# A gated dilated convolution on one core: another order of the matmul groups in even and odd units, and a tail with early row transposes, ScalarE casts and a split last store

## The chip, the cores and the metric

The kernel runs on one core of one Trainium2 chip. The metric is the device time of one execution in microseconds (us), as the median of several runs. The profile is of one more execution, with its own time.

## The reference

Two sequences of 16000 steps with 144 channels go through a causal convolution with 15 taps two steps apart (`pad` is 28, `dil` 2), which gives 288 channels. The first 144 pass through tanh, the last 144 through a sigmoid, the two are multiplied, and the product is multiplied by a 144 x 144 matrix.

```python
B, T, D, K = (2, 16000, 144, 15)     # x [B,T,D], w [K,D,2D], w_o [D,D], bfloat16
dil = 2
pad = (K - 1) * dil
xp = jnp.pad(x, ((0, 0), (pad, 0), (0, 0)))
h = jnp.einsum('btc,cd->btd', xp[:, pad:pad + T, :], w[0])
for i in range(1, K):
    off = pad - i * dil
    h = h + jnp.einsum('btc,cd->btd', xp[:, off:off + T, :], w[i])
f = h[..., :D].copy()
g = h[..., D:].copy()
z = jnp.tanh(f) * _sigmoid(g)
return z @ w_o
```

## The kernel before, in words

**Tiling.** The 32000 steps are cut into 128 pieces of 250, one for each partition of an output tile. Eight neighbouring steps of all pieces make an octet ("oct", `o`); octets are handled in pairs `o0`, `o1`, 15 pairs, and each pair in two units, one for each parity `r`. So 30 units make the main loop (lines 1257 to 1288); even `u` is `r` = 0. The channels are split into 128 (tiles named XA, and V, DU, DD, GX, GU, GV, GD, made from it by subtractions on VectorE) and 16 (XB, BD, packed eight taps to a tile). The 15 taps are not computed one by one: sums and differences of tiles and weights share products between neighbouring outputs. Every matmul of the convolution has 288 output columns and one PSUM bank as its target.

**The parts of a unit**, with their names in `ORDER`. A unit holds banks in pairs.

- CV, CD, XC, XR and SR (lines 973 to 1048) compute for the next unit (`v` = `u` + 1) what its outputs have in common. CV starts a bank with a common product and ScalarE copies the bank (line 967); CD adds to it, and ScalarE evicts it to UD or UC. XC starts a bank and copies it, XR adds to it; its first half (k = 0) is read by VectorE (line 994, into a table kept in Xp), its second half (k = 1) by ScalarE into XS. SR starts the pair of banks p for each of the two octets (h = 0, 1).
- UP (line 1002) adds XS and UC on GpSimd (Pool) into UX.
- EF(u, h) (line 1050) adds the products of GV to the pair p, and VectorE then adds (line 1068) the tables to it: with Xp into a new pair n (k = 0), with UX back into p (k = 1).
- DD(u, h, k) (line 1071) adds six or five products of GD and BD to n (k = 0) or p (k = 1). `halves` then has ScalarE write sigmoid and tanh of the two banks to TG, and VectorE multiplies them (`gate`, line 848). In all units but the last the product goes to Z, both k at once, in `finish`.
- PJ is one of the projections that wait in `todo` (line 913): the octet in Z has been transposed to ZT by a DMA from SP's queue (`ship`, line 908), matmuls with the output matrix (WOR, line 925) make its rows, ScalarE casts them into OS (line 929), and SP stores the octet (line 935). An octet has three groups.

**The tail.** The last unit's gates cannot wait for a transposing DMA. For the last two octets, positions 0, 2, 4 and 6 come from the unit before; they are transposed by DMA and projected by `project_some` (line 938). The last unit's gates go to ZL, a zero-padded area in Xr, and `ship_pair` (line 873) takes two positions at a time (`dl` 7 stands for 5 and 7, `dl` 3 for 1 and 3): three TensorE transposes (line 880), a copy to SBUF (ZTL, in Xr, line 883, helper line 871), three matmuls (line 885), a cast into OS (line 889, helper line 871). `store_some` (line 894) stores an octet.

**What sets the order.** Nothing runs in the order of the calls. Each call adds an operation with an engine, a modelled duration, what it reads and writes, and its place in the list (its index). A planner (`schedule`, line 110, and `run`, line 152) then fills the engines in model time and fixes each engine's order. TensorE takes, of the operations that are ready, the one with the lowest index, no further ahead than `PE_WIN` operations; operations marked `floating` come after all others. An operation that opens a bank may do so only if enough of the eight banks are left for openers with lower indices (`may_open`, line 193). The other engines rank by how late an operation may be by the passes before. SP's queue and its DMAs are planned in the same way. `ORDER` has two strings, for even and odd units, which say in which order the calls are made, and so the indices. `soft` makes an operation start no earlier than another has started, in the plan alone.

Of the kernel before, what the change touches and what calls it, by code (L numbers as in the profile page):

```python
# [5 lines left out]
ACT = mybir.ActivationFunctionType  # L6
# [4 lines left out]
NP = 128  # L11
# [4 lines left out]
PE_WIN = 42  # L16
ORDER = ("EF0 PJ DD00 EF1 XC1 DD01 CV DD10 CD0 XC0 CD1 DD11 XR0 SR0 PJ SR1 PJ XR1 UP0 UP1", "EF0 PJ EF1 XC1 CV DD01 DD00 XC0 CD0 CD1 DD10 SR0 DD11 XR1 XR0 UP0 UP1 SR1 PJ PJ")
# [357 lines left out]
def _conv_wavenet_kernel(nc, x, w, w_o, out):  # L375
    B, T, D = x.shape
# [18 lines left out]
    NPAIR = NOCT // 2  # L395
# [19 lines left out]
    with contextlib.ExitStack() as st:  # L415
# [4 lines left out]
        Xr = sb("Xr", [NP, NX, XCH, D], BF16)  # L420
# [417 lines left out]

        def halves(b, b2, s, k):

            for h, fn in enumerate((ACT.Sigmoid, ACT.Tanh)):
                def th(a, h=h, fn=fn):
                    return evict(a, TG, NTG * 8 * D, ((s * 2 + h) * 4 + 2 * k) * D, D, b, b2, (1 - h) * D, fn)
                g.add("act", th, r=[("bank", b), ("bank", b2)], w=[("TG", s, k, h)], dur=0.31, prio=0)

        def gate(s, k, n, dst, key, dur):

            g.add("dve", lambda v: v.tensor_tensor(dst(), TG[:, s, 1, 2 * k:2 * k + n, :], TG[:, s, 0, 2 * k:2 * k + n, :], ALU.mult),  # L848
                  r=[("TG", s, q, h) for q in range(k, k + n // 2) for h in range(2)], w=key, dur=dur, lock=True)
# [17 lines left out]
        tl_n = [0]  # L867
        last_store = {}

        def cast(eng, dst, src):  # L870
            return (lambda e: e.activation(dst(), src(), ACT.Copy)) if eng == "act" else (lambda e: e.tensor_copy(dst(), src()))  # L871

        def ship_pair(o, h, dl, eng):

            q = tl_n[0] % 4
            os_ = (o + 1) % NO
            tl_n[0] += 1
            pa, bo = _Bank(), _Bank()
            c0 = h * 672 + (dl - 3) // 2 * D
            g.add("pe", [lambda t, i=i: t.transpose(PSb[:, pa.phys * 1024 + 128 * i:pa.phys * 1024 + 128 * i + 128], ZL[:, c0 + 128 * i:c0 + 128 * i + 128], ID[:]) for i in range(3)],  # L880
                  r=[("ZL", h, 3), ("ZL", h, 7), "ID"] if dl == 3 else [("ZL", h, 7), "ID"], w=[("bank", pa)], dur=0.2, floating=True)
# [3 lines left out]
            fns = [lambda t, i=i, c=c, w=w, n=n: t.matmul(PS[:, bo.phys * 512 + c:bo.phys * 512 + c + n * D], lhsT=ZTL[:, q, 128 * i:128 * i + 128],  # L885
                                                          rhs=WOR[:, w:w + n, :].rearrange("p a b -> p (a b)"), start=i == 0, stop=True, skip_group_check=True)
                   for i, c, w, n in ((0, 0, 0, 1), (1, 0, 1, 2), (2, D, 3, 1))]
            g.add("pe", fns, r=[("ZTL", q)] + wor_keys, w=[("bank", bo)], dur=0.3, floating=True)
            op = g.add(eng, cast(eng, lambda: bass.AP(OS[:].tensor, (os_ * 8 + dl - 2) * D, [[NO * 8 * D, NP], [2 * D, 2], [1, D]]),
                                 lambda: PS[:, bo.phys * 512:bo.phys * 512 + 2 * D].rearrange("p (a b) -> p a b", a=2)),  # L890
                       r=[("bank", bo)], w=[("OS", os_, dl)], dur=0.4)
            op.deps.add(last_store[os_])

        def store_some(o, dls, step, n, d0):
            os_ = (o + 1) % NO
            def f(e):
                src = bass.AP(OS[:].tensor, (os_ * 8 + d0) * D, [[NO * 8 * D, NP], [step * D, n], [1, D]])
                dst = bass.AP(out_t, (KD + 8 * o + d0) * D, [[L * D, NP], [step * D, n], [1, D]])
                return e.dma_start(dst, src)
            g.add("sp", f, r=[("OS", os_, d) for d in dls] + [("OS", os_, d, h) for d in dls for h in range(2)], w=[], dur=0.5, dma="st", nbytes=NP * n * D * 2)  # L900
# [12 lines left out]
        def project(o, gi):  # L913
# [15 lines left out]
            g.add("act", lambda e: e.activation(OS[:, os_, a:c, :].rearrange("p e d -> p (e d)"), PS[:, bo.phys * 512:bo.phys * 512 + (c - a) * D], ACT.Copy),  # L929
# [8 lines left out]
        def project_some(o, dls, eng):  # L938

            zt, os_ = (o + 1) % NZT, (o + 1) % NO  # L940
            for h, part in enumerate((dls[:3], dls[3:])):
                b = _Bank()
                fns = []
                for i, dl in enumerate(part):
                    for k in range(2):
# [5 lines left out]
                           r=[("bank", b)], w=[("OS", os_, 0, h)], dur=0.05 + len(part) * D / 1200.0)  # L951
# [119 lines left out]
        def DD(u, h, part):  # L1071
# [20 lines left out]
            gate(s, k, 2, lambda: bass.AP(Xr[:].tensor, XCH * D + c, [[NX * XCH * D, NP], [-D, 2], [1, D]]), [("ZL", h, dl)], 0.22)  # L1092

# [285 lines left out]
```

## Time and profile before

| | us |
|---|---|
| median of 3 runs | 310.57 (310.0 to 312.39) |
| the profiled execution | 310.4 |
| its span, first to last instruction | 308.7 |
| busy in the span: TensorE matmuls | 301.6 |
| VectorE | 289.9 |
| ScalarE | 258.4 |
| GpSimd | 99.6 |

PE is TensorE's matmuls, PEld its weight loads, DVE VectorE, ACT ScalarE, POOL GpSimd, SP the engine whose queue ("SPq") issues the DMAs. A row of the timeline has a start in us from the start of the span, a length in us, engine, line, operation, output <- inputs, shapes, count, and in brackets the idle time before it and what ended it. Neighbouring instructions of a kind are merged. A matmul's shown duration (286 ns for 288 columns) includes its way through the pipeline; in a row without waits the next starts 0.12 us after it. So "PE busy" hides small waits, and the number of matmuls in a stretch tells more. Lines in Z, ZL, ZTL and the table of UE appear under the names of the memory they lie in: ZL and ZTL as Xr, UE as Xp.

### The profile page before, as it was taken

Reading aid. Unit: us, or ns where it says so; the run is one execution under the profiler, and the core shown is the slowest. Engines: PE = TensorE matmul, PEld = TensorE weight load, DVE = VectorE, ACT = ScalarE, POOL = GpSimd, SP = SyncE. Lnnn points to the kernel's source line nnn. Section 1 sums busy time; section 2 is a strip of 40 time slices with the busy share of each in tenths; the row PEclk is TensorE's granted clock in tenths of the full one; section 3 lists DMA queues with packets and bytes.
Section 4 is the critical chain, followed back from the end, with each engine's and each line's share of the span. In section 5 each row is a group of like instructions: output and inputs, shape, how many; then the busy total and the mean of one; then the engine's idle time right before and its main releaser. Section 6 shows DMA issues by size and latency. Waiting matters only on the chain.

```text
span 308.7 us, 7536 instructions
## 1 busy us (share of the span) xinstructions
PE 301.6 (98%) x2569; PEld 235.6 (76%) x2569; DVE 289.9 (94%) x652; ACT 258.4 (84%) x812; POOL 99.6 (32%) x89
## 2 busy tenths in 40 slices
PE   7999999999999999999999999999999999999995
PEld 7787677778877788787776788777788877778884
DVE  1999899999999999999999999999999999999864
ACT  3376788988888998888898888899888889888884
POOL 7480332133333223333321333331233332223330
PEclk9999999999999999999999999999999999999999
DMA  7956657789476883757695476739646783372342
GB/s 212 289 123 148 147 161 187 116 168 162 169 153 155 190 220 101 156 183 170 124 235 165 121 157 173 205 84 236 179 113 146 161 211 99 101 173 71 86 118 115
DMA packets 100241, 48.48 MB, mean 157 GB/s; under 512 B 88269, under 2 KB 90893, under 8 KB 100203
## 3 DMA queue, kind: packets, MB, share of 16 engines
q1 hardware_dynamic: 99657, 47.62, 62.8%
q0 software_dynamic: 512, 0.33, 0.5%
q8 instruction: 20, 0.33, 0.5%
q14 instruction: 18, 0.15, 0.2%
q10 hardware_dynamic: 34, 0.05, 0.1%
HBM read 13.77 MB, written 10.20 MB: 78 GB/s over the span
## 4 chain that ended last, share of the span: by engine, by line
PE 82%; DVE 6%; ACT 4%; SPq 3%; DMA 2%; issue 1%; POOL 0%; DVEq 0%; ACTq 0%
PE PS L823 73%; PE PS L925 9%; DMA WA<-in_w_dram 2%; ACT TG L475 1%; ACT PS L967 1%; SPq L708 1%; DVE V L731 1%; SPq L517 1%; DMA XB<-s 1%; DVE DD L731 1%; DVE DU L731 1%; DVE OS L871 1%; POOL UX L1004 0%; DVE WC L666 0%; SPq L696 0%
## 5 line engine op out<-in xcount | busy, mean ns | idle before, releaser
L1004 POOL TENSOR_TENSOR UX<-UC,XS 128x576 f32<-128x576 f32 x60 | 83.7, 1417 | 194.0 <-ACT UC L478 149.4
L823 PE MATMUL PS<-WA,GD 128*128 128x288 bf16 x450 | 87.6, 286 | 0.2
L967 ACT ACTIVATE PS<-PS 128x288 f32<-128x288 f32 x213 | 80.1, 433 | 0.4
L475 ACT ACTIVATE TG<-PS 128x288 bf16<-128x288 f32 x170 | 60.6, 422 | 15.9 <-PE PS L823 15.8
L823 PE MATMUL PS<-WB,BD 128*128 128x288 bf16 x240 | 67.5, 286 | 0.0
L929 ACT ACTIVATE OS<-PS 128x432 bf16<-128x432 f32 (+1 forms) x88 | 41.8, 491 | 13.6 <-PE PS L925 13.2
L823 PEld LDWEIGHTS PS<-WA,GD 128*128 128x128 bf16 x450 | 40.8, 98 | 16.0 <-DVE PS L1068 3.3
L1068 DVE TENSOR_TENSOR PS<-PS,Xp 128x288 f32<-128x288 f32 x120 | 49.4, 457 | 1.9 <-PE PS L823 0.5
L1068 DVE TENSOR_TENSOR PS<-PS,UX 128x288 f32<-128x288 f32 x120 | 49.3, 455 | 0.0
L823 PE MATMUL PS<-WS,GU 128*128 128x288 bf16 x210 | 44.6, 286 | 0.4 <-DMA XB<-XB 0.2
L994 DVE TENSOR_TENSOR Xp<-PS,UD 128x576 f32<-128x576 f32 x60 | 42.7, 750 | 2.1 <-ACT UD L478 1.7
L925 PE MATMUL PS<-WOR,ZT 128*128 128x144 bf16 (+1 forms) x322 | 41.1, 253 | 0.0
L478 ACT ACTIVATE TG<-PS 128x144 bf16<-128x144 f32 x160 | 33.8, 311 | 5.1 <-PE PS L823 5.0
L823 PE MATMUL PS<-WB,XB 128*128 128x288 bf16 x140 | 37.6, 286 | 0.0
L823 PE MATMUL PS<-WC,GV 128*128 128x288 bf16 x210 | 35.7, 286 | 0.3 <-ACT PS L967 0.3
L925 PEld LDWEIGHTS PS<-WOR,ZT 128*128 128x128 bf16 x322 | 27.9, 98 | 5.5
L823 PE MATMUL PS<-WD,DD 128*128 128x288 bf16 x210 | 31.0, 286 | 0.0
L848 DVE TENSOR_TENSOR Z<-TG 128x576 bf16<-128x576 bf16 (+1 forms) x63 | 27.5, 438 | 2.9 <-ACT TG L478 2.0
L823 PEld LDWEIGHTS PS<-WB,BD 128*128 128x128 bf16 x240 | 23.5, 98 | 5.7
L823 PEld LDWEIGHTS PS<-WS,GU 128*128 128x128 bf16 x210 | 20.4, 98 | 7.3 <-ACT PS L967 1.9
L823 PEld LDWEIGHTS PS<-WD,DD 128*128 128x128 bf16 x210 | 19.7, 98 | 6.5 <-ACT PS L967 1.3
L823 PE MATMUL PS<-WT,DU 128*128 128x288 bf16 x120 | 24.5, 286 | 0.0
(93 smaller groups left out, 476.2 us busy)
## 6 DMA issues: line engine op xcount, KB each, us to landing
out_dram<-OS SPq DMA_DIRECT2D x31, 288.0 KB, 2.6
Xr<-in_x_dram SPq DMA_DIRECT2D x15, 576.0 KB, 4.7
XB<-XB SPq DMA_DIRECT2D x30, 192.0 KB, 2.7
XB<-s SPq DMA_DIRECT2D x59, 32.0 KB, 2.2
s<-T SPq DMA_DIRECT2D x30, 32.0 KB, 2.3
WA<-in_w_dram SPq DMA_DIRECT2D x2, 288.0 KB, 5.0
ZT<-Z SPq DMA_TRANSPOSE x32, 2.9
Xp<-in_x_dram SPq DMA_DIRECT2D x2, 252.0 KB, 4.6
```

The lines of the kernel that those rows point to most:

```text
L475: return e.activation(bass.AP(t[:].tensor, off + (0 if st > 0 else n), [[row, NP], [st, 2], [1, n]]), bass.AP(PS[:].tensor, lo * 512 + c0, ...
L478: ins = e.activation(bass.AP(t[:].tensor, off + i * n, [[row, NP], [1, n]]), bass.AP(PS[:].tensor, q.phys * 512 + c0, [[8 * 512, NP], [1, ...
L517: return e.dma_start(tile_ap, src)
L731: return g.add("dve", lambda v: v.tensor_tensor(dst(), a(), b(), ALU.subtract), r=r, w=wk, dur=dur, prio=2, lock=True)
L823: return lambda t: t.matmul(bank(b), lhsT=lhs(), rhs=rhs(), start=start, stop=True, skip_group_check=True)
L848: g.add("dve", lambda v: v.tensor_tensor(dst(), TG[:, s, 1, 2 * k:2 * k + n, :], TG[:, s, 0, 2 * k:2 * k + n, :], ALU.mult), r=[("TG", s, ...
L925: return t.matmul(PS[:, c0:c0 + n * D], lhsT=ZT[:, zt, blk_, :], rhs=WOR[:, wi_:wi_ + n, :].rearrange("p a b -> p (a b)"), start=first, st ...
L929: g.add("act", lambda e: e.activation(OS[:, os_, a:c, :].rearrange("p e d -> p (e d)"), PS[:, bo.phys * 512:bo.phys * 512 + (c - a) * D], ...
L967: g.add("act", lambda e: e.activation(bank(c), bank(b), ACT.Copy), r=[("bank", b)], w=[("bank", c)], dur=0.29, prio=prio)
L994: return v.tensor_tensor(ue(u % NU, q, 0, 2).rearrange("p (v n) -> p v n", v=2), src, UD[:, u % NUD, :, :], ALU.add)
L1004: op = g.add("pool", lambda p: p.tensor_tensor(UX[:, u % NU, h, :, :], UC[:, 0, :, :], bass.AP(XS[:].tensor, h * N2, [[2 * N2, NP], [0, 2] ...
L1068: g.add("dve", lambda e, dst=dst, src=src, ua=ua: e.tensor_tensor(bank(dst), bank(src), ua(), ALU.add), r=[("bank", src), ("UX", us, h) if ...
```

## The change

The strings of `ORDER` are replaced, and `PE_WIN` goes from 42 to 50. The three row transposes and the copy to SBUF leave `ship_pair` and become `ship_rows`, which is called right behind each gate of the last unit; its copies are all on VectorE, and neither transposes nor projections are `floating` any more. The casts of `project_some` and `ship_pair` of o0 go to ScalarE and those of `ship_pair` of o1 to VectorE; the last group of the third-to-last octet's projection (octet 28) goes from ScalarE to VectorE. `project_some` splits its four positions 2 and 2 instead of 3 and 1, and its casts start, in the plan, no earlier than the last eight `halves`. The last octet is stored in two pieces of four steps. Some modelled durations change too.

```diff
-PE_WIN = 42
-ORDER = ("EF0 PJ DD00 EF1 XC1 DD01 CV DD10 CD0 XC0 CD1 DD11 XR0 SR0 PJ SR1 PJ XR1 UP0 UP1", "EF0 PJ EF1 XC1 CV DD01 DD00 XC0 CD0 CD1 DD10 SR0 DD11 XR1 XR0 UP0 UP1 SR1 PJ PJ")
+PE_WIN = 50
+ORDER = ("EF0 PJ EF1 XC1 CV CD0 XC0 CD1 XR0 DD00 SR0 XR1 PJ DD11 UP0 DD01 PJ UP1 SR1 DD10", "EF0 PJ EF1 DD00 XC1 CV CD0 DD01 CD1 XC0 DD10 XR1 UP0 SR0 DD11 PJ XR0 UP1 SR1 PJ")
...
+        lasts = []
...
-                g.add("act", th, r=[("bank", b), ("bank", b2)], w=[("TG", s, k, h)], dur=0.31, prio=0)
+                lasts.append(g.add("act", th, r=[("bank", b), ("bank", b2)], w=[("TG", s, k, h)], dur=0.31, prio=0))
...
-        def ship_pair(o, h, dl, eng):
-
-            q = tl_n[0] % 4
-            os_ = (o + 1) % NO
-            tl_n[0] += 1
-            pa, bo = _Bank(), _Bank()
+        def ship_rows(h, dl):
+
+            q = 2 * h + (dl == 3)
+            pa = _Bank()
             c0 = h * 672 + (dl - 3) // 2 * D
             g.add("pe", [lambda t, i=i: t.transpose(PSb[:, pa.phys * 1024 + 128 * i:pa.phys * 1024 + 128 * i + 128], ZL[:, c0 + 128 * i:c0 + 128 * i + 128], ID[:]) for i in range(3)],
-                  r=[("ZL", h, 3), ("ZL", h, 7), "ID"] if dl == 3 else [("ZL", h, 7), "ID"], w=[("bank", pa)], dur=0.2, floating=True)
-            old = set(g.readers[("Xr", 0)])
-            a = g.add(eng, cast(eng, lambda: ZTL[:, q, 0:384], lambda: PSb[:, pa.phys * 1024:pa.phys * 1024 + 384]), r=[("bank", pa)], w=[("ZTL", q)], dur=0.4)
-            a.deps |= old
+                  r=[("ZL", h, 3), ("ZL", h, 7), "ID"] if dl == 3 else [("ZL", h, 7), "ID"], w=[("bank", pa)], dur=0.2)
+            a = g.add("dve", lambda e: e.tensor_copy(ZTL[:, q, 0:384], PSb[:, pa.phys * 1024:pa.phys * 1024 + 384]), r=[("bank", pa)], w=[("ZTL", q)], dur=0.27)
+            a.deps |= set(g.readers[("Xr", 0)])
+
+        def ship_pair(o, h, dl, eng):
+
+            q = 2 * h + (dl == 3)
+            os_ = (o + 1) % NO
+            bo = _Bank()
...
-            g.add("pe", fns, r=[("ZTL", q)] + wor_keys, w=[("bank", bo)], dur=0.3, floating=True)
+            g.add("pe", fns, r=[("ZTL", q)] + wor_keys, w=[("bank", bo)], dur=0.25)
...
-                       r=[("bank", bo)], w=[("OS", os_, dl)], dur=0.4)
+                       r=[("bank", bo)], w=[("OS", os_, dl)], dur=0.37 if eng == "dve" else 0.29)
...
+            eng = "dve" if (o, gi) == (2 * NPAIR - 2, 2) else "act"
...
-            for h, part in enumerate((dls[:3], dls[3:])):
+            for h, part in enumerate((dls[:2], dls[2:])):
...
-                           r=[("bank", b)], w=[("OS", os_, 0, h)], dur=0.05 + len(part) * D / 1200.0)
+                           r=[("bank", b)], w=[("OS", os_, 0, h)], dur=0.05 + len(part) * D / 1200.0, soft=lasts[-8:])
...
             gate(s, k, 2, lambda: bass.AP(Xr[:].tensor, XCH * D + c, [[NX * XCH * D, NP], [-D, 2], [1, D]]), [("ZL", h, dl)], 0.22)
+            ship_rows(h, 7 if k == 0 else 3)
...
-        project_some(o0, (0, 2, 4, 6), "dve")
-        ship_pair(o0, 0, 7, "dve")
-        ship_pair(o0, 0, 3, "dve")
-        store_some(o0, [0, 3, 7], 1, 8, 0)
+        project_some(o0, (0, 2, 4, 6), "act")
+        ship_pair(o0, 0, 7, "act")
+        ship_pair(o0, 0, 3, "act")
+        store_some(o0, [3, 7], 1, 8, 0)
+        ship_pair(o1, 1, 7, "dve")
+        ship_pair(o1, 1, 3, "dve")
         project_some(o1, (0, 2, 4, 6), "act")
-        ship_pair(o1, 1, 7, "act")
-        ship_pair(o1, 1, 3, "dve")
-        store_some(o1, [0, 3, 7], 1, 8, 0)
+        store_some(o1, [7], 1, 4, 4)
+        store_some(o1, [3], 1, 4, 0)
```

More of the change, by code (lines that the diff above doesn't have):

```diff
@@ L866, in _conv_wavenet_kernel @@
         ZTL = Xr[:, 0, :, :].rearrange("p e d -> p (e d)")[:, 0:2048].rearrange("p (q c) -> p q c", q=4)
-        tl_n = [0]
         last_store = {}
@@ L899, in f @@
                 return e.dma_start(dst, src)
-            g.add("sp", f, r=[("OS", os_, d) for d in dls] + [("OS", os_, d, h) for d in dls for h in range(2)], w=[], dur=0.5, dma="st", nbytes=NP * n * D * 2)
+            g.add("sp", f, r=[("OS", os_, d) for d in dls] + [("OS", os_, 0, d // 4) for d in dls], w=[], dur=0.5, dma="st", nbytes=NP * n * D * 2)
         def ship(o, keys=None):
```

2 lines of the change are left out of this document (1 added, 1 removed).

## The prediction

> **What bounds the kernel now.** I read the page's busy table first, then the busy time by stretches, then who waits for whom, and last the timeline of the end.
>
> ```profile
> span 308.7 us, 7536 instructions
> ...
> PE 301.6 (98%) x2569; PEld 235.6 (76%) x2569; DVE 289.9 (94%) x652; ACT 258.4 (84%) x812; POOL 99.6 (32%) x89
> ```
>
> TensorE (PE) and VectorE (DVE) are both near the whole span. An average hides where, so next come stretches: a unit without stalls, ten units in a row, the last fifteen, the first four, and the steady part as a whole (columns: PE, PEld, DVE, ACT, POOL busy us, then clock).
>
> ```profile
> 70.88:79.83 8.95, 8.95 (x78) 7.21 (x77) 8.95 (x21) 7.96 (x26) 2.53 (x3) 1.00 0.92 208
> 160.68:170.14 9.46, 9.42 (x78) 6.61 (x77) 9.46 (x23) 8.01 (x27) 2.85 (x3) 1.00 0.58 156
> 70.88:160.68 89.80, 89.80 (x762) 71.14 (x761) 88.80 (x196) 80.08 (x263) 27.69 (x21) 1.00 0.70 168
> 160.68:297.18 136.50, 136.27 (x1143) 105.17 (x1142) 131.57 (x289) 121.06 (x392) 41.93 (x31) 1.00 0.57 144
> 34.74:70.88 36.14, 35.82 (x298) 27.31 (x296) 35.77 (x79) 31.14 (x98) 11.76 (x9) 1.00 0.73 161
> ...
> 60.00:280.00 220.00, 219.77 (x1850) 171.12 (x1849) 217.54 (x477) 195.60 (x635) 68.25 (x49) 1.00 0.66 160
> ```
>
> A count includes two matmuls that overlap the borders, so a unit is 76. The fastest unit needs 8.95 us for them, and unit 14 needs 9.46 for the same 76: that difference, 0.51 us, is stall, although PE "busy" reads 9.42. Ten units at 8.95 would be 89.5 (they took 89.80), fifteen 134.25 (136.50), and the first four, with 296 matmuls, 296/76 x 8.95 = 34.86 (36.14). So stall that an order of work could remove is 0.3 + 2.25 + 1.28 = 3.8 us in all. The clock is 1.00 throughout. DVE is idle only 220 - 217.54 = 2.46 us between 60 and 280: it is as full as PE. What the weight loads waited for in that stretch:
>
> ```profile
> PEld PS L823 <- DVE PS L1068: 3.0, 12, 0.4
> PEld PS L823 <- ACT PS L967: 2.5, 11, 0.3
> ```
>
> Twelve waits are for the PSUM adds of EF (line 1068), eleven for ScalarE's bank copies (line 967). Then the end:
>
> ```profile
> 300.08 2.25 ACT L475 ACTIVATE TG<-PS 128x288 bf16<-128x288 f32 x7 [0.69 <-PE PS L823]
> ...
> 301.59 0.29 PE L823 MATMUL PS<-WB,BD 128*128 128x288 bf16 x1
> ...
> 302.22 0.41 ACT L929 ACTIVATE OS<-PS 128x288 bf16<-128x288 f32 x1
> ...
> 302.51 0.42 ACT L475 ACTIVATE TG<-PS 128x288 bf16<-128x288 f32 x1
> 302.54 0.61 DVE L871 CAST OS<-PS 128x432 bf16<-128x432 f32 x1 [0.20 <-PE PS L947]
> ...
> 303.06 0.35 DVE L871 COPY Xr<-PS 128x384 bf16<-128x384 bf16 x1
> ...
> 303.13 0.50 PE L880 MATMUL PS<-ID,Xr 128*128 128x128 bf16 x6
> 303.33 0.30 DVE L848 TENSOR_TENSOR Xr<-TG 128x288 bf16<-128x288 bf16 x1
> ...
> 303.73 0.33 PE L880 MATMUL PS<-ID,Xr 128*128 128x128 bf16 x3
> 303.81 0.66 DVE L871 CAST OS<-PS 128x144 bf16<-128x144 f32 x2
> ...
> 304.39 0.35 DVE L871 COPY Xr<-PS 128x384 bf16<-128x384 bf16 x1
> ...
> 304.79 0.42 PE L885 MATMUL PS<-WOR,Xr 128*128 128x144 bf16 x3 [0.16 <-DVE Xr L871]
> 305.13 0.94 SPq L899 DMA_DIRECT2D out_dram<-OS  x2
> 305.25 0.46 DVE L871 CAST OS<-PS 128x288 bf16<-128x288 f32 x1
> ```
>
> The last DD matmul ends at 301.59 + 0.29 = 301.88. From there one chain runs: sigmoid, tanh (ends 302.93), gate (303.33), three row transposes (303.73), copy to SBUF (304.39), three projection matmuls (304.79), last cast (ends 305.71), store, end at 308.7. Three places in it are not dependence but queue. The last tanh stands behind a projection eviction (302.22). The last gate, whose input was there at 302.93, stands behind two DVE casts (302.54, 303.06) until 303.33. The last copy, whose transposes ended at 303.73 + 0.33 = 304.06, stands behind two more DVE casts (303.81) until 304.39.
>
> **The change part by part: the end.** The profiled execution took 310.4 us, 1.7 more than its span; the median of the runs is 310.57, so the two stand within 0.2. I sum against 310.4.
>
> Each term is a start on that chain.
>
> The eviction at 302.22 goes to DVE (only for octet 28, third group). Seven halves took 2.25 us, so one step is (2.25 - 0.41)/6 = 0.31: the last tanh could end near 302.93 - 0.29 = 302.64. In the last unit DD00 also moves ahead of DD01; its adds come first on DVE, so the first halves can start a little before 300.08. That is worth nothing more, since the last pair still waits for 301.88.
>
> Against that, the row transposes are no longer "floating" (taken only when nothing else is ready): they rank ahead of later DDs. Six of them took 0.50 us with 0.22 of it one matmul's own tail (219 ns in a row below), so (0.50 - 0.22)/5 = 0.056 each and 0.17 per gate. Two gates are done before the last DD (their DVE rows would start before 301.5), so 0.34 us goes in front of the last DD matmul. Tanh then ends at about 302.95, as now.
>
> The gate: the copies of earlier rows are already done, and the o0 casts are on ScalarE; it starts at 302.97, 0.36 earlier. Transposes start 0.40 later as now (303.73 - 303.33): 303.37. The copy follows by 0.33 instead of 0.66: 303.70. Projection 0.40 on (304.79 - 304.39): 304.10. Cast 0.46 on: 304.56, ending 305.02. It ended 305.71, so 0.69 is gained up to the store.
>
> What the move loads on ScalarE: two casts from project_some(o0), two from ship_pair(o0) and two from project_some(o1), which are asked to wait until the last halves have started.
>
> ```profile
> L871 DVE CAST OS<-PS 128x288 bf16<-128x288 f32 x3 | 1.4, 451 | 0.1
> L871 DVE COPY Xr<-PS 128x384 bf16<-128x384 bf16 x3 | 1.0, 348 | 0.0
> ...
> L871 ACT ACTIVATE OS<-PS 128x288 bf16<-128x288 f32 x1 | 0.4, 410 | 0.1
> ...
> L880 PE MATMUL PS<-ID,Xr x12: 219/219/219, 302.5 to 303.8; 128*128 128x128 bf16 x12
> ```
>
> Six casts by 0.31 (the step) end at 302.95 + 1.86 + 0.1 = 304.9; by 410 ns each, at 305.4. DVE's last cast ends at 305.02, so by the first price ScalarE is just hidden, by the second it sets the end 0.4 later. I take the step price, because the seven halves of the same width ran at it back to back. The Trainium skill's page "ScalarE: Activation LUTs", section "Rules for kernel authors", speaks against this part: plain elementwise work belongs on VectorE, up to about 3x faster. The rows disagree for these PSUM sources, 410 ns on ACT against 451 on DVE, and here the measurement decides.
>
> The last store becomes two of 144 KB.
>
> ```profile
> L899 SPq DMA_DIRECT2D out_dram<-OS x2: 332/332/333, 305.1 to 305.7; - x2
> ...
> DMA to landing us min/median/max: 2.1/2.2/2.3
> ...
> L1324 SPq EVENT_SEMAPHORE  x29: 17/28/28, 306.1 to 308.2; - x29
> ```
>
> A whole store lands 2.1 to 2.3 us after issue, and SP walks through 29 final waits in 2.1 us, so little of a shorter landing can be seen. Bounds: the two stores at 2.1 and 2.3 differ by 0.2 with the later one slower, so 0 to 0.3; I take 0.2. The extra issue (332 ns, and 0.61 between starts, 305.13 to 305.74 from the timeline's 0.94) precedes the last data and is hidden. If the first half were ready only with the second, it would cost that 0.6. The Trainium skill ("DMA: Bandwidth & Descriptors", "Rules for kernel authors") says of transfers to disjoint halves of the partitions not to bother, as they serialize; by a like reading the split gains 0, and the sum is 0.2 worse. Its fit ("Anatomy of one DMA") of 2.0 us plus bytes over 436 GB/s makes half a store 0.34 cheaper, an estimate from that page.
>
> End in all: 0.69 + 0.2 = 0.9. Worst bound 0.3 (ScalarE sets the end, no store gain), best 1.3 (transposes find idle slots: + 0.34).
>
> **The change part by part: the order.** It adds and removes no matmul, eviction, add or DMA; it changes priorities in the planner's list. How far does a string reach? Unit 27 is odd, and its string has XC1 and CV ahead of all DDs:
>
> ```profile
> 280.14 0.65 PE L823 MATMUL PS<-WC,GV 128*128 128x288 bf16 x4
> 280.63 0.41 PE L823 MATMUL PS<-WA,GD 128*128 128x288 bf16 x2
> ...
> 282.71 0.41 PE L823 MATMUL PS<-WT,DU 128*128 128x288 bf16 x2
> 282.95 0.41 PE L823 MATMUL PS<-WT,XA 128*128 128x288 bf16 x2
> ```
>
> Yet DDs (WA,GD) ran from 280.63 on and XC1 (WT,DU) only at 282.71. The reason is in the code: after both EFs, four pairs of PSUM banks are open, all eight, and XC1 cannot open one until a DD has been evicted. So the new strings, which also begin with both EFs, will give much the same run of DDs. What is new: in even units one DD (DD10) has the lowest rank, behind SR1, and can fill a hole while a copy or an eviction is awaited; CD and XR come earlier, so the Pool adds (UX) get their inputs earlier. Both work against the 23 waits above. What is late next: with DD10 at the end, its halves, its gate and the octet's transpose to ZT on SP come later; for the last even unit the transpose now issued at 297.4 lands 2.8 later at 300.2.
>
> ```profile
> L908 SPq DMA_TRANSPOSE ZT<-Z x3: 1275/1294/1343, 287.4 to 297.4; - x3
> ...
> DMA to landing us min/median/max: 2.8/2.8/3.0
> ```
>
> Its reader, project_some, runs after 301.88, so there is 1.7 us of cover. Behind that transpose on SP stand only stores. A lookahead of 50 for 42 costs nothing by itself.
>
> No row shows the new order; the bounds are a gain of 3.8 us (every stall gone, which DVE's 2.46 us of idle in the steady part cuts to about 2.46 + 1.28 = 3.7) and a loss of 0.5 us per unit that stalls as unit 14 does. DVE is full either way, and the 12 waits for its adds come from DVE being late, not from PE's order. I take -0.5, near the zero that the equal work suggests, with a lean to gain from the filler.
>
> Sum: 310.4 - 0.9 - 0.5 = 309.0.
>
> **The rivals.**
> - The order removes most stalls: half of 3.8 beyond my term and the end at its best. 310.4 - 1.1 - 2.5 = 306.8. For it: the 11 waits for copies are what a filler hides. Against: DVE has only 2.46 us to give.
> - The order makes new stalls (the other side). Place: DD10, held back, keeps its pair of banks through the unit, so CV, XC0 and SR0 share six, and wait for ScalarE evictions, as 11 waits do now. Price 0.5 per unit stalled as unit 14. Against the end's 0.9 it decides from two such units on; if ten of thirty stall, 310.4 - 0.9 + 5 = 314.5; if five, 312.0. Against it: ScalarE is busy 195.60 of 220, so it has room, and DD10 may be taken whenever nothing else is ready.
> - The end gains nothing: ScalarE's six casts at 410 ns set it and the two stores share the DMA. 310.4 - 0.3 = 310.1, with the order at zero. For it: 29 final waits cover a shorter landing.
>
> **How the numbers follow.** Forecast 309.0: 0.58, its own range 308.0 to 310.2. Large gain: 0.16. New stalls: 0.16. End gains nothing: 0.10. A difference of 1% is about what a measurement of this kernel can tell from no change: 307.5 and 313.7 are the limits. Faster by over 1%: nearly all of the large gain and a little of the forecast, 0.18. Slower: half of the new stalls, 0.08. Within 1%: 0.74. The range leaves out the outer part of the two middle rivals: 306.8 to 311.9.
>
> **What would show it.** The end: the last gate starts within 0.1 us of the last tanh; from the last DD matmul to the end of the span about 6.0 us (now 308.7 - 301.88 = 6.8); ScalarE has six casts of line 871 and DVE's last cast is of 128x288. The order: the stretch of thirty units is shorter by some tenths, and waits for lines 967 and 1068 fall below 3.0 and 2.5 us. I am wrong if these waits grow, if the last store waits for ScalarE, or if the units shorten by over 2 us.

## The result and the profile after

| | before | after |
|---|---|---|
| median, same chips, 22 runs each, us | 311.04 | 311.94 |
| ratio, 95% interval | | 1.004 [1.0021, 1.0058] |
| profiled execution, us | 310.4 | 311.48 |
| its span, us | 308.7 | 309.7 |

The change made the kernel slower, by 0.4% (a ratio of mean times, without one execution of the kernel before at a lower granted clock, 315.99 us). The forecast was 1.6 us faster than the time before (309.0 for 310.57), the result is 0.9 slower: the sign was wrong, and the miss is 2.5 us. Lines of the changed kernel are numbered a little higher: 967 is now 972, 994 is 999, 1068 is 1073; a small helper for the casts stands at 872.

The page's first lines, after:

```profile
span 309.7 us, 7488 instructions
...
PE 301.7 (97%) x2569; PEld 236.7 (76%) x2569; DVE 289.5 (93%) x651; ACT 258.6 (83%) x819; POOL 100.9 (33%) x89
```

As many matmuls, as much VectorE work: nothing was added, so the time lies in waits. To find where, I cut the span at the first matmul on GV of a unit (the start of EF), so that each stretch holds the same matmuls in both kernels, but for one or two at its borders. Busy time by such stretches, after: units 4 to 23, 24 to 28, 0 to 3, and from the start of unit 29 to the end (columns as in the prediction: PE, PEld, DVE, ACT, POOL, clock, and then DMA share and GB/s).

```profile
71.44:251.51 180.07, 180.07 (x1523) 142.82 (x1521) 179.27 (x396) 159.72 (x515) 55.45 (x41) 1.00 0.68 165
251.51:298.35 46.84, 45.92 (x382) 34.77 (x381) 40.50 (x88) 40.59 (x138) 14.68 (x11) 1.00 0.48 104
34.57:71.44 36.87, 36.35 (x298) 26.82 (x296) 36.63 (x81) 31.53 (x102) 12.68 (x9) 1.00 0.64 160
298.35:309.75 11.40, 7.68 (x84) 6.38 (x81) 7.00 (x20) 7.00 (x23) 2.27 (x2) 0.99 0.62 132
```

The same stretches before (units 0 to 3 stand in the prediction, 34.74:70.88, 36.14 us):

```profile
251.59:297.18 45.59, 45.50 (x383) 34.64 (x382) 41.75 (x91) 40.57 (x134) 13.96 (x11) 1.00 0.42 107
70.88:251.59 180.71, 180.57 (x1523) 141.66 (x1521) 178.63 (x394) 160.56 (x522) 55.66 (x41) 1.00 0.68 165
297.18:308.70 11.52, 7.87 (x84) 6.29 (x82) 7.29 (x21) 6.37 (x18) 2.34 (x2) 1.00 0.38 128
```

Units 0 to 3 cost 36.87 - 36.14 = 0.73 more, units 4 to 23 gave 0.64, units 24 to 28 cost 46.84 - 45.59 = 1.25, and the end, which was to give 0.9, gave about 0.1. Unit 0 began 0.17 earlier. So the 1.07 us of longer span are a loss at both ends of the loop, a gain in its middle, and an end that hardly moved. What weight loads waited for in units 24 to 28, after and then before (us, times, longest):

```profile
PEld PS L823 <- DVE PS L1073: 1.6, 4, 0.7
PEld PS L823 <- ACT PS L972: 1.2, 3, 0.5
```

```profile
PEld PS L823 <- DVE PS L1068: 1.4, 5, 0.4
PEld PS L823 <- ACT PS L967: 0.2, 1, 0.2
```

And from 72 to 251, after and then before:

```profile
PEld PS L823 <- ACT PS L972: 1.2, 5, 0.3
PEld PS L823 <- DVE PS L1073: 0.2, 1, 0.2
```

```profile
PEld PS L823 <- ACT PS L967: 2.1, 9, 0.3
PEld PS L823 <- DVE PS L1068: 1.6, 7, 0.3
```

In the steady part the waits fell from 3.7 to 1.4 us, as the order was to make them do. At both ends of the loop they grew. In units 24 to 28 the waits for ScalarE's bank copies (line 972) went from 0.2 to 1.2 us, and the longest are now 0.7 and 0.5. From 34 to 72, which is units 0 to 3, those for copies went from 1.4 to 2.0 and those for the adds from 0.3 to 0.9.

The end, in the timeline after, from the last DD matmul on:

```profile
302.94 0.29 PE L823 MATMUL PS<-WB,BD 128*128 128x288 bf16 x1
...
303.26 0.71 ACT L475 ACTIVATE TG<-PS 128x288 bf16<-128x288 f32 x2
...
303.92 2.55 ACT L872 ACTIVATE OS<-PS 128x288 bf16<-128x288 f32 x6
...
304.08 0.30 DVE L850 TENSOR_TENSOR Xr<-TG 128x288 bf16<-128x288 bf16 x1
...
304.44 0.34 PE L879 MATMUL PS<-ID,Xr 128*128 128x128 bf16 x3
...
304.82 0.36 DVE L881 COPY Xr<-PS 128x384 bf16<-128x384 bf16 x1 [0.17 <-PE PS L879]
...
305.12 0.41 PE L952 MATMUL PS<-WOR,ZT 128*128 128x144 bf16 x4
...
305.31 0.95 DVE L872 CAST OS<-PS 128x288 bf16<-128x288 f32 x2
305.36 0.41 PE L889 MATMUL PS<-WOR,Xr 128*128 128x144 bf16 x3
305.50 1.63 SPq L903 DMA_DIRECT2D out_dram<-OS  x3
...
305.61 0.41 PE L952 MATMUL PS<-WOR,ZT 128*128 128x144 bf16 x4
```

The tail does what the change says: the gate (304.08) stands 0.11 behind the last tanh (ends 303.97), the copy follows its transposes, and VectorE's last cast ends at 306.26, that is 306.26 - 298.35 = 7.91 after the start of unit 29, where it was 305.71 - 297.18 = 8.53. But the span's end came only 0.1 nearer.

### The profile page after: what moved, and what is told of

Its sections match the earlier page's. It is cut to its first block, busy times and chain, and to the rows that moved or that the text cites. A ratio compares the mean times of both kernels' runs of the same rounds, so it can differ in the third digit from the quotient of the medians.

```text
span 309.7 us, 7488 instructions
## 1 busy us (share of the span) xinstructions
PE 301.7 (97%) x2569; PEld 236.7 (76%) x2569; DVE 289.5 (93%) x651; ACT 258.6 (83%) x819; POOL 100.9 (33%) x89
## 4 chain that ended last, share of the span: by engine, by line
PE 89%; DVE 5%; ACT 3%; issue 1%; POOL 0%; DVEq 0%; POOLq 0%
PE PS L823 77%; PE PS L929 9%; PE PS L590 2%; ACT TG L475 1%; ACT PS L972 1%; DVE PS L1073 1%; DVE V L731 1%; DVE WC L666 0%; ACT TG L478 0%; DVE Xp L999 0%; PE PS L952 0%; PE PS L889 0%; PE PS L618 0%; DVE Z L850 0%; PE PS L879 0%
## 5 line engine op out<-in xcount | busy, mean ns | idle before, releaser
L1009 POOL TENSOR_TENSOR UX<-UC,XS 128x576 f32<-128x576 f32 x60 | 85.1, 1439 | 193.7 <-ACT UC L475 115.8
L972 ACT ACTIVATE PS<-PS 128x288 f32<-128x288 f32 x213 | 81.2, 438 | 0.3
L475 ACT ACTIVATE TG<-PS 128x288 bf16<-128x288 f32 x140 | 50.7, 430 | 13.7 <-PE PS L823 13.5
L872 ACT ACTIVATE OS<-PS 128x432 bf16<-128x432 f32 (+1 forms) x93 | 44.6, 500 | 14.5 <-PE PS L929 14.1
L478 ACT ACTIVATE TG<-PS 128x144 bf16<-128x144 f32 x220 | 46.3, 313 | 8.4 <-PE PS L823 8.2
L823 PEld LDWEIGHTS PS<-WA,GD 128*128 128x128 bf16 x450 | 42.2, 98 | 14.3 <-DVE PS L1073 2.7
```

The costliest lines, as they stand in the source:

```text
L475: return e.activation(bass.AP(t[:].tensor, off + (0 if st > 0 else n), [[row, NP], [st, 2], [1, n]]), bass.AP(PS[:].tensor, lo * 512 + c0, ...
L478: ins = e.activation(bass.AP(t[:].tensor, off + i * n, [[row, NP], [1, n]]), bass.AP(PS[:].tensor, q.phys * 512 + c0, [[8 * 512, NP], [1, ...
L823: return lambda t: t.matmul(bank(b), lhsT=lhs(), rhs=rhs(), start=start, stop=True, skip_group_check=True)
L972: g.add("act", lambda e: e.activation(bank(c), bank(b), ACT.Copy), r=[("bank", b)], w=[("bank", c)], dur=0.29, prio=prio)
L1009: op = g.add("pool", lambda p: p.tensor_tensor(UX[:, u % NU, h, :, :], UC[:, 0, :, :], bass.AP(XS[:].tensor, h * N2, [[2 * N2, NP], [0, 2] ...
```

## The experiments

Two questions: why do units 24 to 28 cost more, and where did the end's 0.6 us go? For the first, the theory at the start was that the new strings of `ORDER` win in the steady part and lose where the loop fills and drains; its rival was that strings and tail don't act separately, because one planner lays out everything. A later, sharper form of the rival: an edit that touches only the last microseconds changes the plan of units far ahead of it. The planner makes ten passes and keeps the best, and each pass ranks operations by a pass backward from the end of the plan before, so this is possible.

The table gives, for each kernel, the lengths of the stretches in us (read as above; the end goes to the last instruction), and the ratio to the kernel before.

| kernel | units 0-3 | 4-23 | 24-28 | end | span | ratio, 95% |
|---|---|---|---|---|---|---|
| before | 36.14 | 180.71 | 45.59 | 11.50 | 308.7 | |
| after | 36.87 | 180.07 | 46.84 | 11.40 | 309.7 | 1.004 [1.0021, 1.0058] |
| order_only | 36.86 | 180.06 | 44.98 | 11.46 | 308.3 | 0.9985 [0.9963, 1.0006] |
| tail_only | 37.54 | 181.43 | 46.12 | 11.50 | 311.2 | 1.0047 [1.0029, 1.0065] |
| middle_new | 36.14 | 186.83 | 45.46 | 12.24 | 316.0 | 1.0251 [1.0197, 1.0305] |
| one_store | 36.86 | 181.99 | 46.85 | 11.10 | 311.8 | 1.0025 [0.9994, 1.0056] |
| loop_kept | 36.87 | 180.06 | 44.97 | 11.41 | 308.6 | 0.9986 [0.9962, 1.0009] |
| old_loop_kept | 36.50 | 180.70 | 45.59 | 11.41 | 309.2 | 1.0015 [0.9987, 1.0042] |
| kept_one_store | 36.87 | 180.07 | 44.98 | 11.10 | 308.1 | 0.9985 [0.9956, 1.0015] |
| kept_few_waits | 36.87 | 180.72 | 44.98 | 10.77 | 309.0 | 0.9984 [0.9961, 1.0008] |
| less_pe | 36.87 | 180.07 | 44.97 | 11.27 | 308.1 | one execution |
| kept_split_few | 36.87 | 180.06 | 44.97 | 10.71 | 307.3 | 0.9964 [0.9934, 0.9994] |
| few_before | 36.14 | 180.70 | 45.59 | 11.33 | 308.3 | 0.9989 [0.9962, 1.0016] |
| one_cast | 36.87 | 180.06 | 46.85 | 11.55 | 309.9 | 1.0081 [1.0049, 1.0113] |

Two kernels with the same queues have the same stretch to 0.02 us, save for a single longer unit among units 3 to 5 in some executions (tail_only's unit 3 took 10.39, one_store's unit 5 10.92, kept_few_waits' unit 5 9.65, old_loop_kept's unit 3 9.36). These come with one execution, not with the plan, and I read nothing from them. The spans start their first unit between 34.5 and 35.7, which is as much scatter again; so stretches, not spans, decide below. They are of one execution each, and the timed ratios cannot tell kernels apart that differ by a few tenths of a us.

### order_only

The kernel before, with the new strings and the lookahead of 50 alone.

```diff
-PE_WIN = 42
-ORDER = (the strings of before)
+PE_WIN = 50
+ORDER = (the strings of after)
```

> The kernel before with the new strings of ORDER and PE_WIN 50, its tail as it was. Theory A (the new strings lose at both ends of the loop): the stretch of units 0 to 3 is again some 0.7 us longer than in the kernel before (36.1), that of units 24 to 28 some 1.2 us longer (45.6), units 4 to 23 some 0.6 us shorter (180.7); time 1.0 to 1.4 us over the kernel before, ratio about 1.004. Rival B (the new tail is what costs, the strings are harmless): ratio 0.998 to 1.000. Rival C (any edit of the list reshuffles the whole plan and moves stalls about, by chance): a stall sum that differs, but in other units than 0, 1, 24, 25 and 26.

The stretches of order_only (units 4 to 23, 24 to 28, 0 to 3):

```profile
71.82:251.88 180.06, 180.06 (x1522) 142.83 (x1521) 179.11 (x395) 159.78 (x519) 55.32 (x41) 1.00 0.69 166
251.88:296.87 44.99, 44.99 (x383) 35.34 (x382) 40.68 (x89) 39.78 (x129) 13.96 (x11) 1.00 0.49 107
34.96:71.82 36.86, 36.34 (x298) 26.83 (x296) 36.52 (x80) 31.53 (x102) 12.69 (x9) 1.00 0.65 160
```

Units 24 to 28 take 44.99 us, all of them with TensorE busy: 0.6 less than before, and 1.85 less than after with the same strings. The loss late in the loop is not the strings' doing. That in units 0 to 3 is: +0.72, as after. In all the order gives 0.72 - 0.65 - 0.61 = -0.54 us up to unit 29 (the loss of 0.72 lies in unit 1, 9.65 us for 8.67); in timed runs the ratio is 0.9985 with an interval that takes in no change.

### tail_only

The changed kernel with the old strings and the lookahead of 42 (the edit above, undone).

> The changed kernel with the old strings and PE_WIN 42: the new tail alone. Theory A: loop as before (unit 29 begins near 297.2), the end 0.15 us earlier measured from there; ratio 0.9985 to 1.000. Rival B: slower than before by about 0.9 us, ratio 1.003. Rival C: the loop's length differs from before by half a us or more in either direction although the strings are the same.

Slower by 0.47%, and units 24 to 28 at 46.12 where the old strings had 45.59, units 4 to 23 at 181.43 for 180.71. The order alone gives -0.5 us, the tail alone is a loss, and neither loss lies in the tail: its own stretch is 11.50, as before. So the two don't add, and the first theory falls.

### middle_new

The changed kernel with the old strings in units 0 to 3 and 24 to 29, and the new ones between.

```diff
-            for t in ORDER[u % 2].split():
+            for t in (ORDER_OLD if u < 4 or u > 23 else ORDER_NEW)[u % 2].split():
```

> The changed kernel with the old strings in units 0 to 3 and 24 to 29 and the new ones in units 4 to 23. Theory A: the loss at both ends goes and the gain of the middle stays, -0.6 -0.15: ratio 0.9975. Rival C: no such addition holds; stalls appear at other places and the ratio is anywhere from 0.997 to 1.004.

The first theory wanted the best of both; it is 2.5% slower, and the slow part is the middle, whose strings are those that ran it in 180.06 elsewhere. Its waits from 70 to 300 us:

```profile
PEld PS L824 <- ACT PS L973: 9.1, 26, 0.7
PEld PS L824 <- DVE PS L1074: 3.7, 9, 1.6
```

Nine us of waits for bank copies: that is the rival "new stalls" of the prediction in full, brought about with the same strings in those units as order_only has. A string fixes indices, not an order; what comes of it depends on the whole plan.

### one_store

The changed kernel with all queues as they are, but the last octet in one store of 288 KB.

```diff
+        s3, s7 = [op for op in g.ops if op.dma == "st"][:-3:-1]
...
+        s3.deps |= s7.deps
...
+        g.ops.remove(s7)
```

> The changed kernel with every queue exactly as planned, but the last octet stored in one piece of 288 KB once all its casts are done, instead of two of 144 KB. Theory A (SP's issues in a row and its 29 final waits set the end, so the split costs): the end of the span comes 0.2 us sooner after the last cast, ratio to before 1.003 against 1.004 for the changed kernel. Rival D (the half store lands sooner and that is worth what I forecast): 0.2 us later than the changed kernel, ratio 1.0045 to 1.005.

From the start of unit 29 to the end it takes 11.10 us for 11.40, so the split in two costs 0.3 as the program stands.

### loop_kept and old_loop_kept

If the loss in units 24 to 28 comes from a new plan of the loop, then the changed kernel with order_only's loop must lose it. In loop_kept the planner must take over order_only's choices, one by one, up to the first operation of the last unit, and is free from there on (KEPT is the list of choices). old_loop_kept is the same with before's own strings and choices.

```diff
+            if n < len(KEPT):
+                op = self.ops[KEPT[n]]
+                e = op.eng
+                st = max(free[e], dict((o, t) for t, o in cands(e))[op])
+            else:
```

> The changed kernel, but its planner must take over, operation by operation, the plan of the order_only kernel up to the first operation of the last unit; only the last unit and the tail are planned anew. Theory E (the new tail costs through the plan: it made the planner arrange units 22 to 26 otherwise, and that is the loss): units 24 to 28 take 45.0 us instead of 46.8, unit 29 begins near 296.9, the end after that takes 11.4 as in the changed kernel, span 308.2 to 308.4, ratio to before 0.998 to 0.999. Rival F (the tail itself costs on the chip): the end takes over 12 us and the ratio is 1.002 or more.

> The new tail behind the old strings, with the kernel before's own plan up to the first operation of the last unit. Theory E: loop as before, unit 29 begins near 297.2, the end 11.35 us (11.50 before): span 308.5, ratio 0.9995. Forecast's sum (the end gains 0.9): ratio 0.997. Rival F: ratio over 1.002.

Units 24 to 28 of loop_kept:

```profile
252.22:297.19 44.97, 44.97 (x382) 35.32 (x381) 40.66 (x89) 39.77 (x129) 13.95 (x11) 1.00 0.49 107
```

The loss is gone, 46.84 to 44.97, with the same tail behind it and the same strings. old_loop_kept keeps before's 45.59. In both the end takes 11.41, so the tail gives 0.1 behind either loop. That they agree to the digit is chance: the planner laid out two different tails, with VectorE's last cast 7.92 and 8.46 into unit 29. The re-planned loop is worth 46.84 - 44.97 = 1.87 us, more than the difference of the two kernels.

### one_cast

Which edit of the tail re-plans the loop? The planner needs no chip, so the program text tells that much: TensorE's order in order_only and in the changed kernel is the same up to about matmul 1841 of 2569 and differs from there. Put singly on order_only, splitting the store, splitting `project_some` 2 and 2 or moving its casts leaves the loop as it was; one line, the cast of octet 28's third group on VectorE, brings about the changed kernel's. That line alone, on order_only:

```diff
-            g.add("act", lambda e: e.activation(...), ...)
+            eng = "dve" if (o, gi) == (2 * NPAIR - 2, 2) else "act"
+            g.add(eng, cast(eng, ...), ...)
```

> order_only with one line of the new tail: the cast of octet 28's third projection group is put on VectorE instead of ScalarE, an operation of the last microseconds. Its five queues, read off line by line, are those of the changed kernel up to the last unit, and differ from order_only's from matmul 1841 of 2569 on. Theory E (it is the plan of units 22 to 26 that costs, whatever brought it about): units 24 to 28 take 46.8 us as in the changed kernel, not 45.0; ratio about 1.004, 1.6 to 2 us over order_only. Rival F (the tail's own work costs): units 24 to 28 stay at 45.0 and the ratio at 0.9985.

Units 24 to 28 of one_cast:

```profile
251.46:298.31 46.85, 45.93 (x383) 34.79 (x382) 40.51 (x88) 40.61 (x138) 14.69 (x11) 1.00 0.50 104
```

46.85, the changed kernel's 46.84, from one cast of 0.41 us that moves to another engine at about 303, while the delays that it brings lie between 259 and 274 us. That is 1.87 us, 0.6% of the whole. The timed ratio to the kernel before is higher, 1.0081 [1.0049, 1.0113], than the 1.0045 to which the stretches of the table add up; the rest is not explained.

The cast is enough to re-plan the loop, but it isn't the only edit with that effect. By the planner, the changed kernel without this line keeps its order of matmuls to the last one. And on order_only, the shorter modelled duration of the row copies alone, or `ship_pair`'s first cast on ScalarE alone, gives the changed kernel's loop too. None of these was run on the chip. So one_cast shows that a small edit of the tail re-plans the loop, and not that this line is the one that did it in the changed kernel.

The planner's model prices the re-plan as well. Its plan ends at 310.4 us for order_only and 312.3 for one_cast, at 311.2 for the changed kernel and 309.3 for loop_kept: 1.9 and 1.8 us, where the chip took 1.87. Against the kernel before it would have misled: the model puts that one at 311.8, so that the change looks 0.7 us faster in it, and the chip has it slower.

### kept_one_store, kept_few_waits, kept_split_few, few_before

Now the end, on loop_kept. kept_one_store has one last store; kept_few_waits also lets SP wait, at the end of the program, only for the four semaphores of the last operations in place of all 29; kept_split_few has the short walk and the split store; few_before is the kernel before with the short walk alone.

```diff
-                for s, v in g.finals:
+                for s, v in g.finals[-4:]:
```

> loop_kept with the last octet stored in one piece. Theory E with the store's cost of 0.3 (11.1 against 11.4 us from unit 29's start to the end): ratio 0.997 to 0.998, 0.3 us below loop_kept. Rival D: 0.2 us above loop_kept.

> kept_one_store, and SP waits at the end only for the four semaphores of the stores instead of for all DMA semaphores; the other transfers have been waited for by their readers. If the walk through 29 waits covers the landing: the end comes as much sooner as the landing leaves, 0.2 to 0.5 us below kept_one_store. If the landing alone sets the end: no change within 0.1 us.

> loop_kept (last octet in two stores) with SP waiting at the end for the stores' semaphores alone. If the split lands sooner once the walk through the waits is gone: from unit 29's start to the end 10.6 us or less, against 10.77 with one store. If it is worth nothing: 10.7 to 10.9. Ratio 0.997 to 0.998 in either case.

> The kernel before with SP waiting at the end for the stores' semaphores alone, nothing else changed. If the walk through 29 waits hides part of the end: from unit 29's start to the end 11.2 to 11.3 us instead of 11.50, ratio 0.999. If not: 11.5 us.

Stores and final waits after (three stores: that of octet o0 and the two pieces of the last one):

```profile
L903 SPq DMA_DIRECT2D out_dram<-OS x3: 332/332/460, 305.5 to 306.7; - x3
...
DMA to landing us min/median/max: 1.8/1.9/2.1
```

```profile
L1331 SPq EVENT_SEMAPHORE  x29: 17/28/28, 307.2 to 309.3; - x29
```

and the final waits of kept_split_few, which no longer outlast the landing (last issue 304.9, landing 1.9 later at 306.8):

```profile
L1336 SPq EVENT_SEMAPHORE  x2: 17/22/28, 306.4 to 306.8; - x2
```

After, the last piece lands at 306.7 + 1.9 = 308.6, but SP is still walking through its waits until 309.3. The walk takes 2.1 us and begins when the last store is issued, so what counts for the end is that issue, not the landing: from the end of the last issue to that of the span it takes 2.6 us in both kernels (308.7 - 306.07 before, 309.75 - 307.13 after). That tells where the end's 0.6 us went. Before, the last store was issued right behind VectorE's last cast and the issue took 0.33. After, the first piece's issue stands there (306.30, behind the cast that ends at 306.26), the second's begins 0.38 later, when the first is done, and takes 0.46, which is 0.13 more: 0.61 - 0.38 - 0.13 = 0.10.

One store saves 0.3 (11.41 to 11.10), and not the whole 0.5, because it also needs ScalarE's last cast, which ends 0.2 after VectorE's; with two stores that cast ends while the first piece is still being issued. With the walk cut the end is 10.77 with one store and 10.71 with two: a further 0.33, and now the split gains, by 0.06. In few_before the walk is worth 11.50 - 11.33 = 0.17. kept_split_few is the fastest by its stretches, and in timed runs 0.9964 [0.9934, 0.9994] of the kernel before.

### less_pe

With the last cast on VectorE only 0.61 us earlier, is it TensorE that holds the chain? In loop_kept, the four matmul groups of `project_some`, four matmuls each, run among the transposes and projections. less_pe runs two of the four in each, and so leaves out half of the partial products.

```diff
+        for op in g.ops:
+            if op.eng == "pe" and len(op.fns) == 4 and op.dur == 0.25:
+                op.fns = op.fns[::2]
```

> loop_kept with every queue as planned, but each of the four project_some groups runs two of its four matmuls: the second partial product of positions 0, 2, 4 and 6 of the last two octets is left out, eight matmuls of 62 ns (0.50 us) on TensorE behind the last DD. Theory G (in the tail TensorE itself is full, so an earlier gate has nothing to make earlier): from the last DD to the last matmul 2.5 us or less instead of 2.80. Rival H (the chain gate, transposes, copy, projection sets the end, as the forecast summed it): 2.7 us or more, no change in the end beyond 0.1 us.

Eight matmuls less, all behind the last DD matmul, at 0.062 each (a group of four takes 0.25 in its row). From the end of the last DD matmul to that of the last matmul it takes 2.56 us for loop_kept's 2.80, and the end 11.27 for 11.41. Removing 0.5 us of TensorE's work at the end gains half of that there and 0.14 at the end, where VectorE's last cast, and with it the first piece's issue, comes 0.12 earlier. So the chain through VectorE and TensorE's own work hold each other up, and neither theory holds alone.

## Why the prediction was wrong, point by point

**The order, forecast -0.5.** Measured by order_only: -0.54 up to unit 29. The reason held in the steady part, fewer waits for copies and adds (3.7 to 1.4 us from 72 to 251). That the size came out is luck: no row gave the -0.5, I had chosen it near zero, and it is the sum of a loss of 0.72 in units 0 to 3, which I had not seen, and a gain of 1.26 behind them.

**The end up to the store, forecast -0.69.** VectorE's last cast came 0.61 earlier against the start of its unit. Step by step: the transposes in front of the last DD matmul cost 0.17 (forecast 0.34; one group of three ran there, ending it 303.23 - 298.35 = 4.88 into the unit for 4.70); the tanh ends 0.74 later than that matmul, the gate and the copy came as forecast (copy 0.74 behind the gate, forecast 0.73). The projection came 0.54 behind the copy instead of 0.40, since four `project_some` matmuls (305.12) stood ahead of it; I had put no TensorE work there. Two slips in my working decide nothing: 302.64 + 0.34 is 302.98 and not 302.95, and the rival with the large gain has the end at 1.1, not at its best of 1.3.

**ScalarE's six casts.** They took 2.55 us, and neither of my prices, 0.31 and 0.41, is what they followed: their starts are 0.42, 0.31, 0.42, 0.50 and 0.50 apart. Ahead of the last two ScalarE idled 0.09 each, waiting for `project_some`'s matmuls, whose last group TensorE began only at 305.61. That is the same TensorE work that I had left out. The estimate "304.9 or 305.4" was for a start at 302.95, 5.77 into the unit; the first cast began at 303.92, 5.57 into it, and the last ended at 306.47, 0.2 behind VectorE's last cast. It did not set the second piece's issue, which began at 306.67 behind the first's; in the kernels with one store it did, by that 0.2. So the rival "the end gains nothing" was right in its size, a gain of 0.1, and in the final waits that cover a shorter landing, and wrong about ScalarE. As for the page "ScalarE: Activation LUTs" of the Trainium skill, its 3x is said of bf16 work such as add and mul, so casts out of f32 banks don't contradict it as the prediction has it.

**The store, forecast -0.2.** The halves landed 1.8 and 1.9 us after their issue, a whole store 2.1 after (2.1 to 2.3 before), so a half is 0.2 to 0.3 quicker. By the fit in the Trainium skill's "DMA: Bandwidth & Descriptors" ("Anatomy of one DMA — SWDGE (gpsimd) path") I had estimated 0.34; it is a fit for DMAs from GpSimd's queue, these are from SP's, and the trace comes near it. But I named the walk through the final waits as a limit and then still counted 0.2 in the sum. The walk covers the whole gain, and the second issue adds to it: +0.3 in place of -0.2. That page's advice against two transfers is about disjoint halves of the partitions, and these are halves of the steps; not to split was right here as the program stands, for the reason of the second issue, and with the walk cut the split was worth 0.06.

**The step that failed.** These are misses of 0.1 to 0.8 us: the end was to give 0.9 and gave 0.1, the order was to give 0.5 and did. The sign was lost in the sum itself: I added the end (a matter of the last 12 us) and the order (a matter of the loop) as if each edit stayed where it was made. Under "The change part by part: the end" I moved the cast at 302.22 to VectorE "only for octet 28, third group" and counted what it does there, and so with every other edit of the tail. They re-planned the loop (that cast alone is enough), and units 24 to 28 took 1.87 us more (loop_kept against the changed kernel, one_cast against order_only). A term for this stood at nothing in my sum; with it the sum is -0.54 + 1.87 - 0.10 = +1.23 us. I wrote that ORDER changes "priorities in the planner's list", and did not ask what a change of the list's end does to it.

**What the re-plan does.** Unit 24 after, where ScalarE's bank copy stands behind its evictions:

```profile
258.13 0.41 PE L823 MATMUL PS<-WT,DU 128*128 128x288 bf16 x2
...
258.33 0.76 ACT L478 ACTIVATE UD<-PS 128x288 f32<-128x288 f32 x2
...
258.92 0.77 ACT L478 ACTIVATE UC<-PS 128x288 f32<-128x288 f32 x2
...
259.50 0.80 ACT L972 ACTIVATE PS<-PS 128x288 f32<-128x288 f32 x2
...
260.06 0.42 PE L823 MATMUL PS<-WS,GU 128*128 128x288 bf16 x2 [0.17 <-ACT PS L972]
...
260.91 1.41 DVE L999 TENSOR_TENSOR Xp<-PS,UD 128x576 f32<-128x576 f32 x2
...
262.24 0.82 DVE L1073 TENSOR_TENSOR PS<-PS,Xp 128x288 f32<-128x288 f32 x2
...
262.75 0.42 PE L823 MATMUL PS<-WA,GD 128*128 128x288 bf16 x2 [0.43 <-DVE PS L1073]
```

The same place in order_only:

```profile
257.54 0.41 PE L823 MATMUL PS<-WT,DU 128*128 128x288 bf16 x2
257.55 1.08 ACT L967 ACTIVATE PS<-PS 128x288 f32<-128x288 f32 x3
...
258.45 0.73 ACT L475 ACTIVATE XS<-PS 128x576 f32<-128x576 f32 x1
...
259.08 0.71 ACT L478 ACTIVATE UD<-PS 128x288 f32<-128x288 f32 x2
```

In order_only XC0 (WT,DU) starts 257.54 - 251.88 = 5.66 into the unit, and ScalarE copies its bank, the third copy from 257.55, ahead of XS, UD and UC. After, XC0 starts 258.13 - 251.51 = 6.62 into the unit. Its copy comes behind UD and UC, XR0 waits for it (260.06), the table of UE follows (260.91), the adds of EF behind the table (262.24), and the next DDs behind the adds (262.75, 0.43 idle). VectorE's own queue stands in this chain too: it runs GV (line 817) until 260.98, right ahead of the table. TensorE starts its next matmul 0.46 us after the one before it at 259.60 and 0.72 at 262.03, where 0.12 is the usual step: 0.33 + 0.60 = 0.93, half of the 1.87. Six more such gaps, up to 273.92, sum to 1.04, and order_only has 0.10 of gaps in these units. This is the loss that the rival "new stalls" described, TensorE waiting for ScalarE, in three units (24 to 26) instead of ten. It is not the mechanism that the rival gave: DD10, which was to hold banks, had its products done by 256.3, and whether XC0 came late for want of a bank is not shown. That this chain is how the plan loses time is read from the trace; that the plan is what loses it was shown by loop_kept and one_cast.

The new tail does not need this plan. order_only's plan is its fifth pass, the best of ten; none of the changed kernel's ten passes comes upon that loop, and the best, the sixth, ends at 311.2 in the model. loop_kept, which has the same tail behind that loop, ends at 309.3. So the search missed a plan that was better by its own measure, and which edit makes it miss is chance.

**Forecasts of what would show it.** The gate within 0.1 us of the tanh, six casts on ScalarE and the 128x288 last cast of VectorE came. From the last DD matmul to the end it took 309.75 - 303.23 = 6.5 us for the forecast 6.0. Waits in the steady part fell, but thirty units shorter "by some tenths" failed: up to unit 29 the loop is 1.34 us longer. I had said I would be wrong "if these waits grow", which they did at both ends of the loop, or "if the last store waits for ScalarE", which it did not: it waited for the issue before it.

## What to carry to other kernels

In a kernel with a planner that lays out all engines at once, an edit is not local: one cast in the last microseconds cost 1.87 us, lost 30 to 44 us ahead of it. Sum the plan's change as a term of its own with both signs; compare the plans first, since the planner's model had 1.8 of it without the chip (though not the sign of the whole change); and test an edit by holding the rest of the plan fixed. Cut the spans at matched instructions, because a stretch repeats to 0.02 us where spans differ by 1. At the end of a kernel, look at what the last queue still does after its last store: a shorter transfer gains nothing under a longer walk of waits.

## What was unexpected in the hardware

GpSimd's add UX takes 1.41 us nearly always (before: 60 of them between 1.40 and 1.69), but up to 2.48 us after:

```profile
L1009 POOL TENSOR_TENSOR UX<-UC,XS x60: 1397/1408/2482, 35.5 to 299.2; 128x576 f32<-128x576 f32 x60
```

The 2.48 us one began at 259.77, when VectorE ran these beside it:

```profile
259.37 0.68 DVE L731 TENSOR_TENSOR V<-XA 128x1024 bf16<-128x1024 bf16 x1
...
259.97 0.42 DVE L694 COPY STA<-Xr 128x1024 bf16<-128x1024 bf16 x1
...
260.30 0.68 DVE L817 TENSOR_TENSOR GV<-V 128x1024 bf16<-128x1024 bf16 x1
```

The next add, at 262.22 beside the PSUM adds of lines 999 and 1073, took 1.40 again. The Trainium skill's "SBUF — State Buffer", section "SBUF: two separate sides", says that VectorE and GpSimd share one pair of ports, which a VectorE operation with two SBUF inputs, or in a fast two-port mode, or GpSimd's own operation locks for its whole length, whichever starts first. The trace agrees: 2.48 - 1.41 = 1.07 us lost where such an operation ran first, none beside those with a PSUM input. And an add that began at 36.87, ahead of a DD subtraction (line 731), took 1.40 while the subtraction took 1.14, for 0.69 on average. The slow add cost nothing at this place, since VectorE waited for nothing from 255 to 276. No run here took the two causes, two inputs and the fast mode, apart.
